# Block-sparse attention and a top-2 mixture of experts: starting the first attention tile head pair by head pair, with the first value sums moved and more value buffers

## The chip, the cores and the metric

One core of one Trainium2 chip (trn2). The metric is device time in microseconds (us) of one execution of the whole program, as the median of three runs.

## The reference

Attention over 4 batches, 8 heads, 768 positions of 64: each query sees its window of keys and, beside it, one summary key (a maximum) and one summary value (a mean) for each block of 32 positions. Its output feeds a router that sends each of the 3072 positions to two of eight experts.

```python
k_sum = k.reshape(B, H, nb, block, D).max(axis=3)
v_sum = v.reshape(B, H, nb, block, D).mean(axis=3)
mask_l = np.abs(pos[:, None] - pos[None, :]) < window
scores_all = np.concatenate([scores_l_m, scores_s], axis=-1)
a = np.exp(scores_all - np.max(scores_all, axis=-1, keepdims=True))
a = a / (np.sum(a, axis=-1, keepdims=True) + 1e-09)
attn_out = np.matmul(a, np.concatenate([v, v_sum], axis=2))
...
h = np.maximum(x[mask] @ w1[e], 0.0)
out[mask] += top2_w[mask, k, None] * (h @ w2[e])
```

## The kernel before, in words

The 3072 positions are 24 tiles of 128 queries, six to a batch. The order of all instructions is written by hand: a loop over t from -2 to 22 (about line 1060 on) issues in each turn, in this order, the scores of tile t + 2 (`mask_sums`, `scores`: TensorE, L308 and L318), their maxima (`smax`: VectorE, L325), the transposes of tile t + 1's exponentials (`p_trans`: TensorE, L341, copied out of PSUM by ScalarE at L344), the exponentials of tile t + 2 (`sexp`: ScalarE, L330 and L333), the product of tile t's weights with the values (`av`: TensorE, L354), the transposes of tile t - 1's output (`x_pe`, L378, copied by `x_copy`, L384), and the division by the sums (`norm`: VectorE, L363 to L369). `at(t, f, ...)` hangs further work between these steps, and `run` issues it: loads of later batches, key maxima, value sums, router and weights. Each engine works through its own list in that order, so an instruction that waits holds up all that is behind it on its engine.

Names that matter here:
- `KB[b % 2]` holds a batch's keys. Batch 0's come in four transfers, one for each pair of heads (L147), behind the queries of tile 0 (`load_q(0)`). `k_head` takes a pair's block maxima (VectorE, L237); later batches' maxima are taken in six pieces (`k_piece`, L231).
- `KX[t % 3]` holds what a tile's scores multiply with: its window of keys (`kx_local`: ScalarE at L122 for tiles 0 and 1, GpSimd at L124 for the others) and the summary keys (`kx_sum`, L130).
- `v_sums(b)` makes a batch's summary values: 48 matrix products in two passes of fp32 (L257), four copies out of PSUM on VectorE (L265 or L267), and for batch 0 copies on GpSimd that put the 24 summary rows into value tiles (L273, L275). `v_rest(b)` fills the others by DMA. For batch 0 it hangs at -0.9, behind tile 0's transposes.
- A tile has two value tiles, one for each half of its queries: one from `VE` (loaded by `load_ve`, L143), and one from `VD` (loaded by `v_load`, L290). `VD` has three buffers in a batch, so `v_load(3)` stands in the loop and waits until tile 0's value product has read the first.
- `warm_up` issues small matrix products whose result nobody reads (L246): `WARM = 100` of them at the start, and 15 between tile 0's transposes.
- SyncE (SP) issues the loads of queries, keys and values, one behind the other. Its transfers use eight semaphores in rotation, so each waits at its issue until the one eight places earlier has landed.

Of the kernel before, what the change touches and what calls it, by code (L numbers as in the profile page):

```python
# [8 lines left out]
F32 = mybir.dt.float32  # L9
# [32 lines left out]
QA = 5  # L42
WARM = 100
SK = HP * NK
# [19 lines left out]
def attn_moe(ctx, tc, qt, kt, vt, wgn, noise, w1, w2, out):  # L64
# [49 lines left out]
    def kx_local(t):  # L114
        b, j = divmod(t, TS)
        k = KB[b % 2][:, :, j * P:j * P + 64 + W]
        n = HP // 2 if t < 1 else HP
        for h in range(0, HP, n):
            for blk in range(2):
                x, y = KX[t % QN][:, h:h + n, blk, L0[blk]:L0[blk] + W], k[:, h:h + n, 64 * blk:64 * blk + W]  # L120
                if t < 2:
                    nc.scalar.activation(x, y, AF.Copy)  # L122
                else:
                    nc.gpsimd.tensor_copy(x, y)  # L124

    def kx_sum(t):
        b, j = divmod(t, TS)
        if j < QN:
            x = KX[t % QN].rearrange("p h b k -> p h (b k)")[:, :, W:W + 2 * NB]
            (nc.gpsimd if b else nc.vector).tensor_copy(x.rearrange("p h (b n) -> p h b n", b=2),  # L130
                                                        KM[b][:, :, None, :].to_broadcast([P, HP, 2, NB]))

    def q_piece(t):
# [4 lines left out]
    VE = [flat[0][:, :TS * VB].rearrange("p (j c) -> p j c", j=TS), keep.tile([P, TS, VB], F32, name="ve")]  # L138
    VD = [[flat[1][:, VB * j:VB * (j + 1)] for j in range(3)],
          [keep.tile([P, VB], F32, name=f"vd{j}") for j in range(2)] + [flat[1][:, 3 * VB:4 * VB]]]  # L140

    def load_ve(b, j):
        nc.sync.dma_start(VE[b % 2][:, j].rearrange("p (h d) -> p h d", h=H), vt[b, j * P:(j + 1) * P])  # L143

    load_q(0)
    for h in range(HP):
        nc.sync.dma_start(KB[0][:, h, PAD:PAD + S], kt[0, :, h])  # L147


# [84 lines left out]
    def k_head(h):  # L234
        if h == 0:
            KM[0] = work.tile([P, HP, NB], F32, name="kmax")
        nc.vector.tensor_reduce(KM[0][:, h], KB[0][:, h, PAD:PAD + S].rearrange("p (n i) -> p n i", i=BLK),  # L237
                                axis=AX.X, op=OP.max)

# [10 lines left out]
    def v_sums(b):  # L250
        if b:
            pt = psum.tile([P, HP, P], F32, name="pt", bufs=2).rearrange("p a b -> p (a b)")
        else:
            pt = psum.tile([P, 2, 512], F32, name="o")[:, 0]
        for j in range(TS):
            for g in range(4):
                nc.tensor.matmul(pt[32 * g:32 * g + NB, 0:C4], ind[:, j, :], VE[b % 2][:, j, C4 * g:C4 * g + C4],  # L257
                                 start=(j == 0), stop=(j == TS - 1), skip_group_check=True)
        x, y = VE[b % 2][W:W + NB], [z[0:NB] for z in VD[b % 2]]
        for g in range(4):  # L260
            i, o = pt[32 * g:32 * g + NB, 0:C4], slice(C4 * g, C4 * g + C4)
            if b == 3 and g % 2:
                nc.scalar.activation(x[:, 0, o], i, AF.Copy)
            elif b:
                nc.vector.tensor_copy(x[:, 0, o], i)  # L265
            else:
                nc.vector.tensor_copy(x[:, 0, o], i)  # L267
        if b == 1:
            nc.gpsimd.tensor_copy(y[0], x[:, 0])
        if b == 0:  # L270
            for i in range(4):
                if i:
                    nc.gpsimd.tensor_copy(x[:, i], x[:, 0])  # L273
                if i < 3:
                    nc.gpsimd.tensor_copy(y[i], x[:, 0])  # L275

    def v_rest(b):
# [3 lines left out]
        if b:  # L281
            for y in VD[b % 2][b == 1:]:
                nc.sync.dma_start(y[0:NB], x[:, 0])
# [3 lines left out]
    def v_load(t):  # L287
        b, j = divmod(t, TS)
        y = VD[b % 2][j % 3].rearrange("p (h d) -> p h d", h=H)
        nc.sync.dma_start(y[NB:NB + VR], vt[b, P * j + 64:P * j + 64 + VR])  # L290
        VX[t] = [VE[b % 2][:, j].rearrange("p (h d) -> p h d", h=H), y]
# [19 lines left out]

    def scores(t):
        s, q, k = SC[t], QR[t], KX[t % QN]
        for hp in range(HP):
            for blk in range(2):
# [20 lines left out]
    def p_trans(t, a):  # L336
        pt = psum.tile([P, HP, P], F32, name="pt", bufs=2)
        for hp in range(HP):
            if t == 0:
                warm_up(1 if a + hp else 8)  # L340
            nc.tensor.transpose(pt[:NK, hp, :], PE_[t][:, a, hp, :], ident)  # L341
# [625 lines left out]

    warm_up(WARM)
    load_q(1)
    for j in range(TS):  # L970
        load_ve(0, j)
    load_q(2)
    v_load(0)
    v_load(1)
    load_q(3)
    v_load(2)
    nc.sync.dma_start(wg32, wgn)
    nc.sync.dma_start(noi, noise)
    load_q(4)
    for h in range(HP):  # L980
        k_head(h)
    q_piece(0)
    q_piece(1)
    at(-0.9, v_sums, 0)
    at(0.8, v_rest, 0)

# [73 lines left out]
    for t in range(-2, NT - 1):  # L1060
# [6 lines left out]
        run(t + 0.03)  # L1067
        if t + 2 < NT:
            mask_sums(t + 2)
            scores(t + 2)  # L1070
# [3 lines left out]
        run(t + 0.5)  # L1074
        if t + 2 < NT:
            smax(t + 2)
        if 0 <= t + 1 < NT:
            p_trans(t + 1, 0)
            p_trans(t + 1, 1)
        if t + 2 < NT:  # L1080
            sexp(t + 2, (0, 1) if t + 3 < NT else (0,))
# [21 lines left out]
        run(t + 0.9)  # L1103
        if 0 <= t and t + 3 < NT:
            v_load(t + 3)
# [598 lines left out]
```

## Time and profile before

| | us |
|---|---|
| median of three runs | 644.94 |
| lowest, highest | 644.83, 646.68 |
| span of the profiled execution | 642.7 |
| the profiled execution's own time | not listed apart; the median is 2.2 above its span |

| engine | busy us, share of the span | instructions |
|---|---|---|
| TensorE (PE) | 621.8 (97%) | 5295 |
| VectorE (DVE) | 481.6 (75%) | 1039 |
| ScalarE (ACT) | 316.0 (49%) | 692 |
| GpSimd (POOL) | 249.0 (39%) | 432 |

The span is the time from the first to the last instruction of one execution that the hardware profiler took. Busy time is a sum over all stages; the attention takes about the first 125 us and the experts the rest. TensorE's busy time has ends that are modelled, so it does not say that TensorE runs at its peak. The times of all rows count from the span's start.

### The profile page before, as it was taken

The page shows a single profiled execution, that of the slowest core. Times are in us where ns is not written, and L with a number is a line of the kernel's source. Part 1 is how long each engine was busy: PE and PEld are TensorE (multiplying, and loading weights), DVE is VectorE, ACT ScalarE, POOL GpSimd, SP SyncE. Part 2 cuts the span into 40 slices and gives each one's busy share as a digit, 9 for nine tenths or more (in the row PEclk, how much of TensorE's full clock was granted, in tenths as well). Part 3 has the DMA queues.
Part 4 walks back from the last instruction along what each step waited for, and adds up shares of the span by engine and source line. Part 5 has one row for each costly group of instructions (what it writes and reads, how often), then busy time and mean ns, then how long its engine had stood idle before and what let it go on. Part 6 is the DMA issues. An engine that isn't in the chain of part 4 may idle for free.

```text
span 642.7 us, 14142 instructions
## 1 busy us (share of the span) xinstructions
PE 621.8 (97%) x5295; PEld 360.3 (56%) x5295; DVE 481.6 (75%) x1039; ACT 316.0 (49%) x692; POOL 249.0 (39%) x432
## 2 busy tenths in 40 slices
PE   8899899899999999999999999999999999999995
PEld 7678777765554554555455544554554455445542
DVE  5848899889797599178878887987898679757510
ACT  4958898852153463065337534654464255425300
POOL 4433044203254433623573256336632542333041
PEclk9989999999999999999999999999999999999999
DMA  9999996678469696636986688779786868763021
GB/s 308 296 294 327 296 303 211 214 265 288 139 200 187 188 221 152 256 91 162 203 245 162 150 212 261 169 139 220 220 199 157 217 202 165 180 193 120 3 95 50
DMA packets 123707, 127.91 MB, mean 199 GB/s; under 512 B 83242, under 2 KB 86674, under 8 KB 123630
## 3 DMA queue, kind: packets, MB, share of 16 engines
q1 hardware_dynamic: 111838, 90.66, 52.9%
q0 software_dynamic: 11792, 36.27, 17.9%
q8 instruction: 43, 0.70, 0.4%
q14 instruction: 34, 0.28, 0.1%
HBM read 81.85 MB, written 25.61 MB: 167 GB/s over the span
## 4 chain that ended last, share of the span: by engine, by line
PE 78%; DVE 11%; ACT 3%; issue 3%; DMA 3%; POOL 0%; POOLq 0%; SPq 0%; DVEq 0%; ACTq 0%
PE pt L1429 29%; PE h L1357 16%; PE h L854 8%; PE pt L909 7%; PE pt L1357 3%; PE o L1357 3%; PE h L909 2%; DVE nm L325 2%; DMA htl<-in_vt_dram 2%; ACT p L333 2%; PE pt L341 1%; PE o L354 1%; PE o L246 1%; PE s L318 1%; DVE y L920 1%
## 5 line engine op out<-in xcount | busy, mean ns | idle before, releaser
L90 POOL DMA_INDIRECT out_dram<-y,tb x52 | 69.3, 1333 | 167.5 <-DVE y L931 129.3
L90 POOL DMA_INDIRECT xg<-xd,tb x54 | 60.4, 1119 | 118.9 <-DVE dsc L653 32.9
L1429 PEld LDWEIGHTS <-hth 128*128 128x128 f16 x576 | 56.4, 98 | 66.7
L931 DVE SCALAR_TENSOR_TENSOR y<-pt,tb,prev 128x512 f32<-128x512 f32 x42 | 31.5, 749 | 65.7 <-PE pt L1429 54.2
L1357 PEld LDWEIGHTS <-w1h 128*128 128x128 f16 x504 | 48.9, 98 | 38.1 <-issue 4.1
L1429 PE MATMUL pt<-w2h,hth 128*128 128x512 f16 x288 | 69.0, 379 | 0.0
L1429 PE MATMUL pt<-w2l,hth 128*128 128x512 f16 x288 | 69.0, 379 | 0.0
L1429 PE MATMUL pt<-w2h,htl 128*128 128x512 f16 x288 | 69.0, 379 | 0.0
L1357 PEld LDWEIGHTS <-w1l 128*128 128x128 f16 x504 | 49.3, 98 | 34.9
L90 POOL DMA_INDIRECT prev<-out_dram,tb x45 | 52.1, 1158 | 24.6 <-issue 12.9
L333 ACT ACTIVATE p<-s,nm 128x120 f32<-128x120 f32 x192 | 50.8, 376 | 0.8
L854 PE MATMUL h<-xte,w1h 128*128 128x384 f16 (+2 forms) x248 | 48.9, 336 | 0.0
L1429 PEld LDWEIGHTS <-htl 128*128 128x128 f16 x288 | 28.2, 98 | 34.0
L1346 ACT ACTIVATE w1h<-stg 128x768 f16<-128x768 f32 (+1 forms) x24 | 22.7, 944 | 40.2 <-DVE stg L1337 40.2
L1389 ACT ACTIVATE hth<-h 128x384 f16<-128x384 f32 (+4 forms) x48 | 23.8, 496 | 35.6 <-PE h L1357 35.6
L1346 ACT ACTIVATE w1l<-stg 128x768 f16<-128x768 f32 (+1 forms) x24 | 22.5, 942 | 37.3 <-DVE stg L1337 37.3
L1357 PE MATMUL h<-xte,w1h 128*128 128x384 f16 (+4 forms) x180 | 39.7, 329 | 0.7 <-DVE h L1383 0.4
L1357 PE MATMUL h<-xte,w1l 128*128 128x384 f16 (+4 forms) x180 | 39.7, 329 | 0.0
L1310 ACT ACTIVATE x<-xt 128x512 f16<-128x512 f32 (+2 forms) x44 | 26.5, 626 | 23.2 <-issue 19.1
L1337 DVE TENSOR_TENSOR stg<-stg 128x256 f32<-128x256 f32 x96 | 36.3, 419 | 0.8
L854 PEld LDWEIGHTS <-w1h 128*128 128x128 f16 x256 | 24.7, 98 | 19.4 <-issue 1.0
L1392 DVE SCALAR_TENSOR_TENSOR htl<-h,hth 128x384 f16<-128x384 f32 (+4 forms) x48 | 26.4, 563 | 11.8 <-ACT hth L1389 11.5
(301 smaller groups left out, 1297.3 us busy)
## 6 DMA issues: line engine op xcount, KB each, us to landing
stg<-in_w_dram SPq DMA_DIRECT2D x64, 512.0 KB
q<-in_qt_dram SPq DMA_DIRECT2D x24, 256.0 KB
xd<-x SPq DMA_DIRECT2D x24, 256.0 KB
out_dram<-xg SPq DMA_DIRECT2D x8, 768.0 KB
kb<-in_kt_dram SPq DMA_DIRECT2D x6, 768.0 KB
hth<-in_vt_dram SPq DMA_DIRECT2D x12, 260.0 KB
htl<-in_vt_dram SPq DMA_DIRECT2D x16, 195.0 KB
ve<-in_vt_dram SPq DMA_DIRECT2D x12, 260.0 KB
```

The source lines that it names most:

```text
L90: return nc.gpsimd.indirect_dma_start(**kw)
L333: nc.scalar.activation(PE_[t][:, a, hp, :], SC[t][:, a, hp, :], AF.Exp, bias=NM[t][:, 1, a, hp:hp + 1], scale=0.125)
L854: nc.tensor.matmul(ph[:, :n], w1_of(w, wn, c, f), x[:, xo + c, c0:c1], start=(k == 0), stop=(k == 11))
L909: nc.tensor.matmul(py, hx[:, f, c * P:c * P + P], wv[:, f, :], start=st, stop=sp)
L931: nc.vector.scalar_tensor_tensor(y, py[:, :d], gw, pv[:, :d], op0=OP.mult, op1=OP.add)
L1310: nc.scalar.activation(t[:r, c:c + k], src, AF.Copy)
L1337: nc.vector.tensor_tensor(o, x, y, op=op)
L1346: nc.scalar.activation(hi, x, AF.Copy, scale=W1S)
L1357: nc.tensor.matmul(ph[:, :h], w[:, la, a, P * j:P * j + P], x[:, j, :h], start=start and k == 0, stop=k == 5, skip_group_check=True)
L1389: nc.scalar.activation(hh[:, f, t], src, AF.Relu)
L1392: nc.vector.scalar_tensor_tensor(hl[:, f, t], src, 0.0, hh[:, f, t], op0=OP.max, op1=OP.subtract)
L1429: nc.tensor.matmul(py, x, wv[:, f, :], start=st, stop=sp, skip_group_check=True)
```

## The change

Seven things change:
- Two pairs of key heads are loaded ahead of tile 0's queries, and the last pair in two halves.
- Tile 0's scores, maxima and exponentials are issued for each head pair (`start`, `start_head`, `start_max`), with its summary keys copied per pair on VectorE. The windows of tile 0 are copied by ScalarE; tile 1's windows and its summary keys, and tile 2's summary keys, go to GpSimd.
- `WARM` falls from 100 to 48; six warm-up products follow each of the first three pairs, and twelve follow tile 2's scores. The 15 between tile 0's transposes go.
- Tile 2's queries are loaded ahead of the values, tile 3's one place earlier.
- `v_sums(0)` moves from -0.9 to 0.1: behind tile 2's scores and tile 1's transposes, ahead of tile 0's value product.
- `VD` has five buffers in batch 0; GpSimd fills all five with the summary rows, eight copies instead of six.
- `v_load(3)` and `v_load(4)` leave the loop and stand at the start, behind tile 4's queries.

```diff
-WARM = 100
+WARM = 48
...
     def kx_local(t):
         b, j = divmod(t, TS)
         k = KB[b % 2][:, :, j * P:j * P + 64 + W]
-        n = HP // 2 if t < 1 else HP
-        for h in range(0, HP, n):
-            for blk in range(2):
-                x, y = KX[t % QN][:, h:h + n, blk, L0[blk]:L0[blk] + W], k[:, h:h + n, 64 * blk:64 * blk + W]
-                if t < 2:
-                    nc.scalar.activation(x, y, AF.Copy)
-                else:
-                    nc.gpsimd.tensor_copy(x, y)
+        for blk in range(2):
+            nc.gpsimd.tensor_copy(KX[t % QN][:, :, blk, L0[blk]:L0[blk] + W], k[:, :, 64 * blk:64 * blk + W])
...
-            (nc.gpsimd if b else nc.vector).tensor_copy(x.rearrange("p h (b n) -> p h b n", b=2),
+            (nc.gpsimd if t else nc.vector).tensor_copy(x.rearrange("p h (b n) -> p h b n", b=2),
...
-    VD = [[flat[1][:, VB * j:VB * (j + 1)] for j in range(3)],
+    VD = [[flat[1][:, VB * j:VB * (j + 1)] for j in (0, 1, 2, 4, 5)],
...
+    VN = (5, 3, 3, 3)
...
-    load_q(0)
     for h in range(HP):
-        nc.sync.dma_start(KB[0][:, h, PAD:PAD + S], kt[0, :, h])
-
+        if h == 2:
+            load_q(0)
+        for c in ((0, S // 2), (S // 2, S)) if h == HP - 1 else ((0, S),):
+            nc.sync.dma_start(KB[0][:, h, PAD + c[0]:PAD + c[1]], kt[0, :, h, c[0]:c[1]])
...
-        nc.vector.tensor_reduce(KM[0][:, h], KB[0][:, h, PAD:PAD + S].rearrange("p (n i) -> p n i", i=BLK),
-                                axis=AX.X, op=OP.max)
+        for n in ((0, NB // 2), (NB // 2, NB)) if h == HP - 1 else ((0, NB),):
+            nc.vector.tensor_reduce(
+                KM[0][:, h, n[0]:n[1]],
+                KB[0][:, h, PAD + BLK * n[0]:PAD + BLK * n[1]].rearrange("p (n i) -> p n i", i=BLK),
+                axis=AX.X, op=OP.max)
+        x = KX[0][:, h].rearrange("p b k -> p (b k)")[:, W:W + 2 * NB]
+        nc.vector.tensor_copy(x.rearrange("p (b n) -> p b n", b=2), KM[0][:, h, None, :].to_broadcast([P, 2, NB]))
+
+    def start_head(h):
+        k_head(h)
+        for blk in range(2):
+            nc.scalar.activation(KX[0][:, h, blk, L0[blk]:L0[blk] + W], KB[0][:, h, 64 * blk:64 * blk + W], AF.Copy)
+        if h == 0:
+            mask_sums(0)
+        scores(0, h, h + 1)
+        if h < HP - 1:
+            warm_up(6)
+        if h:
+            start_max(h - 1)
+
+    def start_max(h):
+        nc.vector.tensor_reduce(NM[0][:, 0, :, h], SC[0][:, :, h], axis=AX.X, op=OP.max)
+        nc.scalar.activation(NM[0][:, 1, :, h], NM[0][:, 0, :, h], AF.Copy, scale=-0.125)
+        for a in range(2):
+            nc.scalar.activation(PE_[0][:, a, h, :], SC[0][:, a, h, :], AF.Exp, bias=NM[0][:, 1, a, h:h + 1],
+                                 scale=0.125)
+
+    def start():
+        NM[0] = work.tile([P, 2, 2, HP], F32, name="nm", bufs=2)
+        PE_[0] = awork.tile([P, 2, HP, NK], F32, name="p")
+        for h in range(HP):
+            start_head(h)
+        start_max(HP - 1)
+        q_piece(1)
...
-            for i in range(4):
-                if i:
+            for i in range(VN[0]):
+                if 0 < i < 4:
                     nc.gpsimd.tensor_copy(x[:, i], x[:, 0])
-                if i < 3:
-                    nc.gpsimd.tensor_copy(y[i], x[:, 0])
+                nc.gpsimd.tensor_copy(y[i], x[:, 0])
...
-        y = VD[b % 2][j % 3].rearrange("p (h d) -> p h d", h=H)
+        y = VD[b % 2][j % VN[b]].rearrange("p (h d) -> p h d", h=H)
...
-            if t == 0:
-                warm_up(1 if a + hp else 8)
...
     load_q(1)
+    load_q(2)
     for j in range(TS):
         load_ve(0, j)
-    load_q(2)
     v_load(0)
+    load_q(3)
     v_load(1)
-    load_q(3)
     v_load(2)
...
-    for h in range(HP):
-        k_head(h)
-    q_piece(0)
-    q_piece(1)
-    at(-0.9, v_sums, 0)
+    v_load(3)
+    v_load(4)
+    at(0.1, v_sums, 0)
...
-        if t + 2 < NT:
+        if t == -2:
+            start()
+        elif t + 2 < NT:
             mask_sums(t + 2)
             scores(t + 2)
...
+        if t == 0:
+            warm_up(12)
...
-        if 0 <= t and t + 3 < NT:
+        if 0 <= t < NT - 3 and t + 3 > 4:
             v_load(t + 3)
```

Three places where rows move. On SP, from tile 4's queries on (q4; `kb1` holds batch 1's keys, `ve` its first value tiles, `htl` the second value tiles of batch 0). Before:

```order
L112 DMA q4_100<-in_qt_dram 128x512
L107 DMA kb1_92<-in_kt_dram 128x4x384
L112 DMA q0_96<-in_qt_dram 128x512
L143 DMA ve_101<-in_vt_dram 128x520 x3
L107 DMA kb1_92<-in_kt_dram 128x4x384
L107 DMA kb0_91<-in_kt_dram 128x4x384
L280 DMA hth_89<-hth_89 24x2x520
L290 DMA htl_90<-in_vt_dram 96x520
```

Now:

```order
L112 DMA q4_100<-in_qt_dram 128x512
L318 DMA htl_90<-in_vt_dram 96x520 x2
L107 DMA kb1_92<-in_kt_dram 128x4x384
L112 DMA q0_96<-in_qt_dram 128x512
L139 DMA ve_101<-in_vt_dram 128x520 x3
L107 DMA kb1_92<-in_kt_dram 128x4x384
L107 DMA kb0_91<-in_kt_dram 128x4x384
L308 DMA hth_89<-hth_89 24x2x520
```

The second value tiles of tiles 3 and 4 have moved ahead of batch 1's keys; tile 3's stood behind all of these.

On TensorE, from tile 0's last transposes (`p_346`, now `p_262`) to tile 0's value product. Before:

```order
L341 MATMUL pt_402<-ident_110,p_346 120x128
L257 MATMUL o_422<-hth_89 24x130 x24
L308 LDWEIGHTS identb_112
L308 MATMUL s_459<-mask0_121,identb_112 64x4x96
...
L318 MATMUL s_459<-kx2_95,q2_98 64x120 x16
L341 MATMUL pt_482<-ident_110,p_412 120x128 x4
L341 MATMUL pt_489<-ident_110,p_412 120x128 x4
L354 MATMUL o_505<-hth_89,pts_400 64x65
```

Now:

```order
L367 MATMUL pt_374<-ident_111,p_262 120x128 x4
...
L336 MATMUL s_392<-mask0_122,identb_113 64x4x96
L346 MATMUL s_392<-kx2_95,q2_98 64x120 x16
L275 LDWEIGHTS identb_113
L275 MATMUL o_191<-identb_113 128x128
...
L367 MATMUL pt_427<-ident_111,p_380 120x128 x4
L367 MATMUL pt_434<-ident_111,p_380 120x128 x4
L286 MATMUL o_450<-hth_89 24x130 x24
L380 MATMUL o_487<-hth_89,pts_372 64x65
```

The value sums (`o<-hth`, 24 rows here, two passes each in the profile) stood ahead of tile 2's mask and scores; now they stand between tile 1's transposes and tile 0's value product.

On GpSimd, the copies of the summary rows (`htl<-hth`, `hth<-hth`) and what stands around them. Before:

```order
L124 COPY kx0_93<-kb0_91 128x4x96 x2
L275 COPY htl_90<-hth_89 24x520
L273 COPY hth_89<-hth_89 24x520
...
L124 COPY kx1_94<-kb0_91 128x4x96 x2
```

Now:

```order
L118 COPY kx1_94<-kb0_91 128x4x96 x2
L124 COPY kx1_94<-kmax_263 128x4x48
L118 COPY kx2_95<-kb0_91 128x4x96 x2
L124 COPY kx2_95<-kmax_263 128x4x48
L118 COPY kx0_93<-kb0_91 128x4x96 x2
L303 COPY htl_90<-hth_89 24x520
...
L303 COPY htl_90<-hth_89 24x520 x2
L118 COPY kx1_94<-kb0_91 128x4x96 x2
```

Tile 1's windows and the summary keys of tiles 1 and 2 have come in ahead, and two summary-row copies more stand before tile 4's windows (`kx1<-kb0`, the last row of both).

## Rows read from the trace of the kernel before

**Rows 1.** Windows: busy us of PE, PEld, DVE, ACT, POOL; PEclk; DMA share; GB/s.
```profile
140.00:160.00 20.00, 20.00 (x137) 11.07 (x135) 18.97 (x64) 5.33 (x11) 6.13 (x11) 1.00 0.89 310
```

**Rows 2.** Chain of waits, 0 to 70 us: start us, us, what.
```profile
1.55 7.41 PE o L246 x100
...
14.46 1.46 PE o L257 x48
...
18.05 1.09 PE o L354 x32
...
21.79 10.41 DMA htl<-in_vt_dram
...
32.25 1.93 PE o L354 x30
34.18 1.05 PE pt L378 x4
...
36.61 1.02 PE pt L341 x8
...
38.72 0.59 PE pt L378 x4
...
40.76 0.29 PE s L308 x4
41.05 0.82 PE s L318 x32
...
42.35 0.90 issue
...
66.33 1.63 issue
```

**Rows 3.** Windows, the start and the stall at tile 3.
```profile
1.50:5.00 3.50, 3.45 (x33) 3.46 (x34) 1.91 (x14) 0.54 (x1) 2.72 (x17) 1.00 0.85 289
5.00:9.00 4.00, 4.00 (x74) 3.90 (x71) 3.56 (x4) 1.51 (x5) 2.62 (x11) 1.00 1.02 388
30.00:32.20 2.20, 0.00 (x0) 0.00 (x0) 2.20 (x5) 2.17 (x9) 0.88 (x3) 1.00 1.03 267
32.20:34.10 1.90, 1.85 (x30) 1.74 (x30) 0.25 (x1) 0.44 (x2) 0.66 (x2) 0.54 1.10 303
34.10:36.60 2.50, 2.50 (x42) 1.92 (x42) 1.06 (x3) 0.60 (x1) 0.00 (x0) 0.67 1.05 270
```

**Rows 4.** Timeline of DVE: start us, us, instruction, count [idle before, releaser].
```profile
6.09 2.91 DVE L237 TENSOR_REDUCE kmax<-kb 128x24 f32<-128x768 f32 x3 [0.39 <-DMA kb<-in_kt_dram]
...
10.53 1.16 DVE L325 TENSOR_REDUCE nm<-s 128x8 f32<-128x960 f32 x1 [1.07 <-PE s L318]
...
15.99 1.21 DVE L267 COPY hth<-o 24x130 f32<-24x130 f32 x4 [3.07 <-PE o L257]
...
27.29 0.69 DVE L231 TENSOR_REDUCE kmax<-kb 128x16 f32<-128x512 f32 x1 [1.26 <-DMA kb<-in_kt_dram]
```

**Rows 5.** Timeline of POOL, the copies of summary rows and what follows them.
```profile
17.32 0.62 POOL L275 COPY htl<-hth 24x520 f32<-24x520 f32 x1 [5.79 <-issue]
...
21.36 2.75 POOL L124 COPY kx<-kb 128x384 f32<-128x384 f32 x6
```

**Rows 6.** Timeline of ACT, exponentials of tiles 0 and 1 and the copies between.
```profile
11.96 2.12 ACT L333 ACTIVATE p<-s,nm 128x120 f32<-128x120 f32 x8
13.92 1.17 ACT L344 ACTIVATE pts<-pt 120x512 f32<-120x512 f32 x2
...
15.22 2.12 ACT L333 ACTIVATE p<-s,nm 128x120 f32<-128x120 f32 x8
```

**Rows 7.** The page's DMA issues: out<-in, engine, count, KB each.
```profile
htl<-in_vt_dram SPq DMA_DIRECT2D x16, 195.0 KB
```

**Rows 8.** Timeline of SP's queue, eight places behind batch 1's last value load.
```profile
36.00 0.35 SPq L373 DMA_DIRECT2D xd<-x  x1
```

**Rows 9.** DMA queues between 64 and 68 us: packets, MB, share of 16 engines.
```profile
q8 instruction: 1, 0.02, 1.8%
```

More of the change, by code (lines that the diff above doesn't have):

```diff
@@ L258, in v_sums @@
                                  start=(j == 0), stop=(j == TS - 1), skip_group_check=True)
-        x, y = VE[b % 2][W:W + NB], [z[0:NB] for z in VD[b % 2]]
+        x, y = VE[b % 2][W:W + NB], [z[0:NB] for z in VD[b % 2][:VN[b]]]
         for g in range(4):
@@ L281, in v_rest @@
         if b:
-            for y in VD[b % 2][b == 1:]:
+            for y in VD[b % 2][b == 1:VN[b]]:
                 nc.sync.dma_start(y[0:NB], x[:, 0])
@@ L310, in mask_sums, with scores @@
                                  skip_group_check=True)
-    def scores(t):
+    def scores(t, h0=0, h1=HP):
         s, q, k = SC[t], QR[t], KX[t % QN]
-        for hp in range(HP):
+        for hp in range(h0, h1):
             for blk in range(2):
@@ L1074, in attn_moe @@
         run(t + 0.5)
-        if t + 2 < NT:
+        if t == 0:
+            warm_up(12)
+        if -2 < t < NT - 2:
             smax(t + 2)
@@ L1079, in attn_moe @@
             p_trans(t + 1, 1)
-        if t + 2 < NT:
+        if -2 < t < NT - 2:
             sexp(t + 2, (0, 1) if t + 3 < NT else (0,))
```

## The prediction

> **What bounds the kernel now.** I read the windows by stage first: between 140 and 160 us TensorE is busy for 20.00 of 20 us [rows 1]. From there on a start that comes earlier by some time should end earlier by about as much. So the question is what the change does to the first 40 us, and whether it survives until 140.
>
> For the first 40 us I read the chain of waits [rows 2]. The reader is to see three things. The 100 warm-up matmuls stand in it for 7.41 us, then tile 0's scores, maxima and transposes follow. The value sums of batch 0 take 1.46 us at 14.46, and straight behind them come mask and scores of tile 2, so that tile 0's value product (L354) starts at 18.05. And the longest piece is a transfer: tile 3's second value tile, 10.41 us from its issue at 21.79 to 32.25. [...]
>
> The profiled execution has no time of its own listed; its span of 642.7 us lies 2.2 us under the median of 644.94, and I put my differences on that median.
>
> **Part 1: tile 0 by head pairs.** The last key head landed when DVE's run of reduces ended: three reduces in 2.91 us from 6.09, so the fourth ran from about 8.05 to 9.00 [rows 4]. The same bytes (four heads and one q tile) still stand ahead of that landing, so it doesn't move. Now DVE has in front of the last half head: the third head (about 7.05 to 8.0), a copy, one head pair's maximum (a quarter of 960 columns; between 0 and the 1.16 us of a whole one, I take 0.4, in proportion with some fixed cost), two half reduces (0.55 each; between 0.48, half of 0.97, and 0.97). That ends at 9.6. Tile 1's sums go to POOL (192 columns; between 0 and the 0.62 of POOL's copy of 520, I take 0.35, in proportion with some fixed cost) [rows 5], so tile 1's scores start at 10.0 and end at 11.2 with mask and scores of 0.29 and 0.82 [rows 2]: as early as before, no more. What moves is tile 0's exponentials: all done at about 11.4, where they ended at 14.08 before (11.96 and 2.12) [rows 6]. Its eight transposes then take 1.02 us behind tile 1's scores, with no warm-ups between them, to 12.3. ACT's copies of them (1.17) end at 13.0. Tile 1's exponentials ended 2.25 behind such copies (15.09 to 17.34), so now at 15.3 against 17.34 [rows 6]. **Gain here: 2.0 us.**
>
> The warm-ups cost nothing. Only 33 matmuls fitted into 1.5 to 5.0 and 74 in the next 4 us [rows 3], so TensorE doubled its rate at about 5; the clock column shows 1.00 in both, I go by the spacing. 48 warm-ups end near 5.9, and q tile 0 lands there as well. Six more behind each of three heads and twelve behind tile 2's scores (0.06 each) run while TensorE would wait for DVE or ACT.
>
> **Part 2: value sums behind tile 2's scores.** TensorE now takes tile 2's scores at 12.3 to 13.5, tile 1's transposes as the exponentials come, to 15.5, then the sums (1.46) to 17.0. Behind them nothing is left to hide what follows: four DVE copies (1.21) to 18.3 and POOL's first copy (0.62) to 19.0 [rows 4, 5]. Before, scores and transposes of tiles 2 and 1 covered just that. Tile 0's value product starts at 19.1 instead of 18.05, TensorE standing idle for 2 us ahead of it. **The 2.0 us are gone and 1.1 more are lost.** POOL makes eight value copies where it made six; at six in 4.04 us (17.32 to 21.36) [rows 5] it is free at 23.8, and tile 4's first keys are there at 24.3, which costs up to 0.2 us more. So tiles 1 and 2 run about 1.2 us later than before.
>
> **Part 3: five buffers.** Tile 3's and tile 4's second value tiles are now issued right behind q tile 4, ahead of batch 1's keys, and have nothing to wait for. The stall at tile 3 goes. TensorE had reached it at 29.9; now it gets there at 30.9 to 31.0 and goes on at once: 1.09 us at full clock, done at 32.0 instead of 34.18, **2.2 us earlier**. What is late next is DMA work put behind the two loads, 390 KB [rows 7] or 1.0 to 1.5 us at the 388 to 267 GB/s shown [rows 3]. DVE's key maximum waited for batch 1's second half until 27.29 [rows 4]; at 28.5 it still ends ahead of tile 3's value product, which needs DVE's norm of tile 2 by 30.9. Batch 1's last value load had landed by 36.00, when SP issued the transfer eight places behind it [rows 8]; it then has one load (195 KB, 0.7 us) more ahead of it, 36.7, and TensorE wants it at about 36.5.
>
> **Part 4: the clock.** Transposes, mask and scores behind the stall took 2.43 us (34.18 to 36.61) where the same took 0.59, 0.29 and 0.82 later [rows 2]: without the fall another 0.7 us. I count half, 0.35, since only one execution shows the fall. DVE takes back 0.25 in front of tile 6's maximum, where batch 2's key maxima stand.
>
> **Sum:** 2.2 + 0.35 - 0.25 = 2.3 us at tile 6. From there to 140 us the order of work is the old one. **Forecast 642.6 us.**
>
> **The rivals.**
> *DMA sets the pace.* The share of the DMA engines is 1.02 to 1.10 in these stretches [rows 3], and the change sends the same bytes. If the last value load of batch 1 had landed just before its use at 39.31 (38.72 and 0.59) [rows 2], the gain is gone: 644.9, up to 0.7 more. Against it stands SP's row at 36.00 [rows 8].
> *The clock falls in the new gap.* TensorE was idle for over 2.2 us when it fell before [rows 3]; the new gap at 17 to 19 us is 2.0. The two slow stretches lost 0.46 of 1.9 and 0.33 of 2.5 us, 1.7 us in all. Put on tiles 0 to 2, it leaves 0.6 of the gain: 644.3. For it speaks the similar length, against it that the sums right before it keep TensorE busy, where before the stall it had little.
> *Slower: instruction fetch.* TensorE stood for 0.90 us at 42.35 and for 1.63 us at 66.33 in the midst of one tile's matmuls, with no releaser but "issue" [rows 2], and around the second the DMA queue that carries instructions moved one packet of 0.02 MB [rows 9]. If such packets stand in line behind full queues, tiles that run closer together meet more of them. It decides from three more stalls of 1.63 on: 642.6 + 4.9 = 647.5. Against it: two in 30 us of full queues. [...]
> *More than forecast.* One of these two stalls goes as TensorE's instructions shift: 641.0, and 640.3 with all of the clock's 0.7.
>
> **How the numbers follow.** Forecast 0.55, DMA 0.17, clock 0.15, fetch 0.08, more 0.05. A difference of 0.3% (1.93 us) is about what a measurement of this kernel can tell from none: faster means under 643.0, slower over 646.9. The forecast's own spread, 641.4 to 643.6 from the bounds of part 1, the half-counted clock and the 1.0 to 1.5 us of DMA, gives 0.46 to faster and 0.09 to same; "more" gives 0.05 to faster, the clock 0.03. DMA goes to same but for 0.01, the clock's other 0.12 to same, fetch to slower: 0.54, 0.37, 0.09. The range leaves fetch and the outer tenth of the rest out: 640.3 to 645.4.
>
> **What would show it.** Right: tile 0's exponentials end near 11.4; a gap of about 2 us between the value sums and tile 0's value product, which starts near 19; no wait at tile 3's; tile 6's scores end near 34. Wrong: L354 of tile 0 starts before 18; a DMA wait at DVE's key maxima or at batch 1's value sums; a granted clock under 1 around 19 us; a gain at 36 us that is no longer there at 140.

## The result, and the profile after

The change takes **649.21 us** (nine runs, 646.85 to 652.35) against 644.94 of nine runs of the kernel before: a ratio of 1.0072, 95% interval 1.0049 to 1.0095. That is 0.7% slower, where the forecast was 642.6. The profiled execution took 648.33 us with a span of 646.6; the span of the kernel before was 642.7. One execution of a later kernel, h1_copy_first, took 1175.36 us at a granted clock of 0.794 and is left out of that kernel's numbers.

The chain of waits of the changed kernel, first 24 us (start us, us, what). L275 are the warm-ups, L346 a head pair's scores, L255 its maximum, L256 and L258 its scaling and exponentials, L245 a key copy, L303 GpSimd's first value copy, L380 a value product:

```profile
1.55 5.08 PE o L275 x48
...
7.56 0.41 PE s L346 x8
...
8.00 0.42 DVE nm L255
...
8.44 0.22 ACT nm L256
...
8.68 0.61 ACT p L258 x2
9.29 0.35 ACT kx L245 x2
9.64 0.05 issue
9.69 0.47 PE s L346 x8
...
10.94 0.61 ACT p L258 x2
11.55 0.35 ACT kx L245 x2
11.90 0.05 issue
11.95 0.50 PE s L346 x8
...
21.89 0.62 POOL htl L303
22.52 0.04 issue
22.56 1.37 PE o L380 x30
```

Follow one turn: the second head pair's scores end at 7.97, then the first pair's maximum, scaling and two exponentials run, then the third pair's key copy, and only then, at 9.69, come the third pair's scores. The fourth's start at 11.95: **2.26 us a head pair**, where VectorE needs 0.97 for a pair's reduction (2.91 for three) [rows 4]. The chain alternates between three engines, one of them at work at a time. ScalarE's rows show where this leaves tile 0 and tile 1 (start us, us, engine, line, operation, in brackets the idle time before and what ended it):

```profile
14.55 0.61 ACT L258 ACTIVATE p<-s,nm 128x120 f32<-128x120 f32 x2
...
16.54 2.12 ACT L361 ACTIVATE p<-s,nm 128x120 f32<-128x120 f32 x8
```

Tile 0's exponentials end at 15.16 and tile 1's at 18.66; before, at 14.08 and 17.34 [rows 6]. TensorE's rows of the next step:

```profile
18.96 1.53 PE L286 MATMUL o<-hth 128*24 128x130 f32 x48
21.83 0.33 PE L380 MATMUL o<-hth,pts 120*64 120x65 f32 x2 [1.33 <-DVE hth L296]
22.56 0.27 PE L380 MATMUL o<-htl,pts 120*64 120x65 f32 x1 [0.40 <-POOL htl L303]
```

The value sums end at 20.49 and tile 0's value product gets going at 22.56, 4.5 us behind the 18.05 of before [rows 2]. Between the two lie 2.07 us; two of the products already run at 21.83, so TensorE stands idle for 1.33 and for 0.40 of them. Windows of the same execution (window, us, busy time and instructions of PE, PEld, DVE, ACT and POOL, granted clock, DMA share, GB/s):

```profile
15.00:20.00 5.00, 5.00 (x100) 4.06 (x104) 1.50 (x2) 4.77 (x16) 0.00 (x0) 1.00 1.09 244
20.00:25.00 5.00, 3.27 (x76) 2.64 (x68) 2.13 (x7) 1.92 (x8) 2.89 (x5) 0.83 1.05 330
25.00:30.00 5.00, 5.00 (x100) 4.20 (x96) 3.50 (x7) 2.98 (x11) 4.73 (x10) 0.83 1.07 353
```

In this execution TensorE's granted clock is 0.83 from 20 to 25 us, where that pause lies, and 0.83 in the 5 us behind; the fall that the kernel before had behind 32 us (0.54 and 0.67) [rows 3] is gone: in those two windows it is 1.00 now. So is the 10.41 us transfer at tile 3 [rows 2]: from 15 to 120 us TensorE waits for no DMA any more, where it waited 2.3 us for this one before.

Two marks tell how far the late start reaches: VectorE's maximum of tile 6 and of tile 23, the last. First the kernel before, then the change:

```profile
36.79 1.16 DVE L325 TENSOR_REDUCE nm<-s 128x8 f32<-128x960 f32 x1 [1.45 <-PE s L318]
...
121.37 1.15 DVE L325 TENSOR_REDUCE nm<-s 128x8 f32<-128x960 f32 x1
```

```profile
38.92 1.15 DVE L353 TENSOR_REDUCE nm<-s 128x8 f32<-128x960 f32 x1
...
121.48 1.16 DVE L353 TENSOR_REDUCE nm<-s 128x8 f32<-128x960 f32 x1
```

2.1 us late at tile 6, level at tile 23. Read from these two executions alone, the late start is absorbed and the loss comes later. One part of it does lie at the very end. The last row of the chain, first of the kernel before, then of the change:

```profile
636.99 0.71 POOL out_dram L90
```

```profile
638.92 0.71 POOL out_dram L90
```

From the end of this transfer to the end of the span it was 5.0 us (637.70 to 642.7) and is now 7.0 (639.63 to 646.6). In the trace's records GpSimd ends the branch around the overflow code (L1679, L1651 before) with a semaphore and drains its queue behind it. Between the starts of the semaphore and of the drain lay 0.09 us before (637.54 and 637.63); 2.59 lie there now (639.47 and 642.06). It is not the branch itself that got longer: from the branch to the semaphore it takes 0.48 us in both. The order of work there is unchanged; GpSimd's program has five instructions more in front of it (764 records against 759). Of the 3.9 us between the two spans, 0.1 thus stand at tile 23's maximum and 2.0 in this tail; the other 1.8 lie between the two (from that maximum to the end of the last transfer it was 516.3 us and is 518.1).

### The profile page after: what moved, and what is told of

It reads as the page before. It is cut to its first block, busy times and chain, and to the rows that moved or that the text cites. A ratio compares the mean times of both kernels' runs of the same rounds, so it can differ in the third digit from the quotient of the medians.

```text
span 646.6 us, 14093 instructions
## 1 busy us (share of the span) xinstructions
PE 621.9 (96%) x5258; PEld 359.6 (56%) x5258; DVE 482.4 (75%) x1044; ACT 316.3 (49%) x697; POOL 252.4 (39%) x438
## 4 chain that ended last, share of the span: by engine, by line
PE 72%; DVE 10%; issue 6%; ACT 5%; POOL 3%; DMA 2%; SPq 1%; POOLq 0%; DVEq 0%; ACTq 0%
PE pt L1457 29%; PE h L1385 16%; PE h L880 5%; PE pt L935 5%; PE o L1385 3%; PE pt L1385 3%; PE h L935 2%; ACT p L361 2%; DVE nm L353 2%; POOL xg L90 2%; PE o L380 1%; PE pt L367 1%; POOL out_dram L90 1%; DMA xg<-xd,tb 1%; PE s L346 1%
## 5 line engine op out<-in xcount | busy, mean ns | idle before, releaser
L361 ACT ACTIVATE p<-s,nm 128x120 f32<-128x120 f32 x184 | 48.7, 376 | 0.8
```

What stands on the lines that cost most here:

```text
L361: nc.scalar.activation(PE_[t][:, a, hp, :], SC[t][:, a, hp, :], AF.Exp, bias=NM[t][:, 1, a, hp:hp + 1], scale=0.125)
```

## The experiments

**Theory A**: the late start is absorbed, and the loss is the position of the code: engines stop for instructions at other places, GpSimd at its jump above all. **Theory B**: the late start carries to the end, and its apparent absorption is chance between two executions. **Theory C**: all of it is chance. Ratios are to runs of the kernel before on the same chip, 95% intervals in brackets.

**e1_pool5: five instructions on GpSimd, nothing else.**

```diff
     nc.gpsimd.memset(XG[3], 0.0)
+    pad = const.tile([P, 4], F32, name="pad")
+    for i in range(5):
+        nc.gpsimd.memset(pad[:, 0:1], 0.0)
```

> The kernel before with nothing but five one-column memsets added on GpSimd while it is idle in the first 10 us, so that GpSimd's program is as much longer as it is in the change (754 + 5 recorded instructions). Theory A (position of the code): the change lost about 2 us in the tail, because GpSimd's jump past the overflow branch then has to wait for an instruction fetch (2.6 us from the branch's last semaphore to the drain where it was 0.1); the same must happen here, and the time is 2.0 us above the kernel before, with the work up to the last matmul unmoved. Theory B (the late start of the change carries to the end): nothing is late here, so the time is that of the kernel before within 0.5 us. Theory C (chance from execution to execution): no difference either.

646.79 us, 1.0023 (1.0002 to 1.0044). The last row of its chain, against a span of 643.6:

```profile
636.18 0.71 POOL out_dram L90
```

6.7 us of tail. The semaphore and the drain lie 2.39 us apart. Five one-column memsets in the first 10 us bring this at 637 us, so GpSimd's number of instructions alone does it (764 records against 759; the expectation's 754 is wrong). The interval of the time reaches down to almost nothing; it is the gap that shows the effect.

**e2_count: the old order with the change's instruction counts.**

```diff
-WARM = 100
+WARM = 63
...
+    for i in range(8):
+        nc.vector.memset(pad[:, 1:2], 0.0)
+    for i in range(6):
+        nc.scalar.activation(pad[:, 2:3], ones[:, 0:1], AF.Copy)
...
+    for i in range(2):
+        nc.sync.dma_start(pad2[0:1, i:i + 1], noise[0:1, 0, i:i + 1])
```

(and e1's five memsets)

> The kernel before, its order of work untouched, with every engine's number of instructions made that of the change before 15 us: 63 warm-up matmuls in place of 100 (TensorE 74 rows fewer), five GpSimd memsets, eight VectorE memsets, six ScalarE copies of one column, two DMAs of one element. Theory A: the stalls of the change at 124 us (about 1 us), at 520 us (about 1.3 us) and in the tail (2 us) come back without its new order: 3 to 4.5 us above the kernel before. Theory B: the start is as early as before, so no difference, 0.5 us at most. Theory C: no difference of its own.

647.84 us, 1.0049 (1.0025 to 1.0073), with a tail of 6.95 us. It falls short of A's range (2.8 us above by the medians, 3 to 4.5 expected) and lies well above B's; its interval overlaps e1's, so that code on the other engines costs anything beside this gap is not shown by it. Its start was also somewhat later than intended (tile 6's maximum at 37.57).

**e3_pool_less: the change, GpSimd's count as before.** Five small constants move to VectorE.

```diff
-    nc.gpsimd.tensor_scalar(base8, base8, HALF, None, op0=OP.subtract)
+    nc.vector.tensor_scalar(base8, base8, HALF, None, op0=OP.subtract)
...
```

(likewise the copy into `bs`, both writes of `tie`, the subtraction on `iotar`)

> The change with five of GpSimd's small constants made by VectorE, so that GpSimd has as many instructions as in the kernel before. Theory A: GpSimd's jump in the tail takes 0.1 us again in place of 2.6, and the time falls by 2.0 us against the change, to about 1.7 to 2.3 us above the kernel before; the stalls at 124 and 520 us stay, unless VectorE's five instructions move one of them. Theory B: five small instructions in the first 4 us change nothing: 0.7% above the kernel before, as the change is.

647.12 us, 1.0034 (1.0009 to 1.0059). The tail is 5.1 us again, semaphore and drain 0.09 apart. So about 2 us of the loss go with that gap, **and about as much stays**: the change has a second cost.

**e4_five: part 3 alone.**

```diff
-    VD = [[flat[1][:, VB * j:VB * (j + 1)] for j in range(3)],
+    VD = [[flat[1][:, VB * j:VB * (j + 1)] for j in (0, 1, 2, 4, 5)],
...
     load_q(4)
+    v_load(3)
+    v_load(4)
```

> The kernel before with part 3 of the change alone: five buffers for the second value tile and both early loads; head pairs, value sums and warm-ups as before. GpSimd makes two more copies (2 instructions more, fewer than the five). Theory A: the stall at tile 3 goes, tile 6's maximum starts about 2 us earlier than in the kernel before, and by 100 us none of this is left, since VectorE is full from 70 to 120 us; at the end between 0.5 us less and 1 us more than the kernel before, by where instruction fetches fall. Theory B: what is gained at tile 6 stays: 1.5 to 2.3 us under the kernel before.

644.85 us, 0.9987 (0.9965 to 1.0009): at most 0.35% faster, perhaps nothing. The stall is gone from its profile, yet nothing that can be measured is gained. Why, e1 and e2 show: they have the old order too. Chain of waits of e1_pool5 at tile 3, then of e2_count:

```profile
25.60 1.08 PE o L357 x30
26.68 1.32 issue
28.00 0.28 PE o L357 x2
```

```profile
22.30 0.74 PE o L358 x21
23.04 10.06 DMA htl<-in_vt_dram
33.10 0.04 issue
33.15 1.15 PE o L358 x30
```

e2 waits for the same transfer as the kernel before; e1, which differs from that kernel in five memsets alone, doesn't: its tile has the value rows in time, and tile 6's maximum starts at 34.60, 2.2 us ahead of the 36.79 of the kernel before. (The 1.32 us in e1 are one of TensorE's stops, told of in the last section.) **The wait that part 3 removes is there in one execution and not in another.**

The next four test the start. f1 delays it with the old code, f2 to f4 undo part 2 and the loop of part 1 in e3, singly and together.

**f1_late.**

```diff
         for i in range(n):
-            nc.tensor.matmul(VO[0][:, i % 2, 0:P], identb, identb, start=True, stop=True, skip_group_check=True)
+            x = ident if n == WARM and i >= 30 else identb
+            nc.tensor.matmul(VO[0][:, i % 2, 0:P], x, x, start=True, stop=True, skip_group_check=True)
```

> The kernel before with 70 of its 100 warm-up matmuls in float32 in place of bfloat16, about 0.07 us longer each, and no instruction more or fewer on any engine: the first scores start about 4 us later, everything behind is as before. Theory A (the start is absorbed by tile 12, since the change was 2.1 us late at tile 6 and level at 100 us): 0 to 1 us above the kernel before. Theory B (a late start carries to the end, and what looked like absorption was one execution of the kernel before against one of the change): 3 to 4.5 us above it.

650.46 us, 1.0112 (1.0079 to 1.0145). The delay came out larger than meant, and the count did move: a float32 matmul is recorded as two, with two weight loads (170 warm-ups in the chain, 140 rows more), and the warm-ups take 19.66 us where they took 7.41 [rows 2], about 0.175 us more for each of the 70 (expected 0.07). Tile 6's maximum starts at 44.75, 8.0 us late, tile 23's 5.3 us late, and the median is 7.3 us up. A has no room for that.

**f2_sums_back.**

```diff
-    at(0.1, v_sums, 0)
+    at(-0.9, v_sums, 0)
...
-        if t == 0:
+        if t == -1:
             warm_up(12)
```

> The change with GpSimd's count as in the kernel before (as in e3_pool_less) and with part 2 undone: batch 0's value sums behind tile 0's transposes again, the twelve warm-ups there too. The pause of 2 us ahead of tile 0's value product goes, and with it the fall of the granted clock at 23 to 27 us; tile 0's product starts 1.5 to 2 us earlier than in the change (22.56), tile 6's maximum as well. Theory A: this is absorbed, time as e3_pool_less (0.3% above the kernel before). Theory B: 1.5 to 2.5 us under e3_pool_less, level with the kernel before.

645.43 us, 1.0024 (1.0004 to 1.0044). Tile 0's value product starts at 20.50, as expected. The granted clock still falls, but earlier (0.66 from 10 to 15 us). The time is nearer to A's 0.3% than to B's, and its interval holds e3's value as well as almost nothing: by itself this run decides nothing.

**f3_kx_pool and f4_both.** f4 is f3 with f2's edit. In both, three writes of `caps` move to VectorE too, so that GpSimd has 760 records.

```diff
-            nc.scalar.activation(KX[0][:, h, blk, L0[blk]:L0[blk] + W], KB[0][:, h, 64 * blk:64 * blk + W], AF.Copy)
+            x, y = KX[0][:, h, blk, L0[blk]:L0[blk] + W], KB[0][:, h, 64 * blk:64 * blk + W]
+            if h < 2:
+                nc.scalar.activation(x, y, AF.Copy)
+            else:
+                nc.gpsimd.tensor_copy(x, y)
...
+        if h:
+            start_max(h - 1)
         scores(0, h, h + 1)
...
-        if h:
-            start_max(h - 1)
```

> e3_pool_less with the loop of tile 0 broken up: key copies of heads 2 and 3 on GpSimd in place of ScalarE, so that none stands behind exponentials, and each head's maximum issued ahead of the next head's scores; part 2 as in the change. If that loop (2.26 us a head) was what held tile 0, its exponentials end at 11.4 to 12.5 in place of 15.16 and tile 0's value product starts near 20 in place of 22.56. Theory A: time as e3_pool_less. Theory B: 2 us under it.

> e3_pool_less with both: loop broken up and value sums back ahead of tile 2's scores. Tile 0's value product starts at 16 to 17, 1 to 2 us ahead of the kernel before (18.05), where the forecast had 19.1 and the change 22.56. Theory A: no faster than the kernel before. Theory B: 1 to 2.5 us under the kernel before, which would make it the fastest of these.

646.24 us, 1.0032 (1.0011 to 1.0053), and 644.93 us, 1.0020 (0.9999 to 1.0041). The loop did not break: tile 0's exponentials end at 15.32 and 14.96, its value product starts at 24.09 and 21.61. TensorE's rows of f3_kx_pool say why (L352 scores, L262 exponentials):

```profile
9.03 0.44 PE L352 MATMUL s<-kx,q 64*64 64x120 f32 x8 [0.99 <-ACT p L262]
...
13.20 0.68 PE L352 MATMUL s<-kx,q 64*64 64x120 f32 x8 [0.77 <-ACT p L262]
```

A head pair's scores wait for the *exponentials of the one before*, which they don't need. All four stand in one PSUM tile (one buffer for TensorE's results), and the dependence holds the tile, not a quarter of it: 0.99 and 0.77 us of idle time in these two rows. The key copies in ScalarE's list were only half of the loop.

**g1_two_tiles: f2 with tile 0's scores in two PSUM tiles.**

```diff
-        NM[0] = work.tile([P, 2, 2, HP], F32, name="nm", bufs=2)
...
+        if h % 2 == 0:
+            SC[0] = gate_space()[:, :, :SK // 2].rearrange("p a (h k) -> p a h k", h=2)
+            S2.append(SC[0])
...
+        nm = work.tile([P, 2, 2, 2], F32, name="nm2", bufs=2)
+        nc.vector.tensor_reduce(nm[:, 0], S2[i], axis=AX.X, op=OP.max)
```

> f2_sums_back with tile 0's scores in two PSUM tiles, heads 0 and 1 in the first, 2 and 3 in the second, each with its own maximum and exponentials. Theory D (in the change and in f3_kx_pool the heads waited for one another because all four stand in one PSUM tile and a dependence holds the tile: a head's scores wait for the exponentials of the head before): tile 0's exponentials end at 11.4 to 12.2, as the forecast had it, in place of 14.9, and tile 0's value product starts near 16 in place of 20.50. About six tenths of a shift at tile 0 have reached tile 23 in the runs so far, so 0.5 to 2 us under the kernel before. Rival E (the landing of the keys, about 1 us a head, or VectorE holds tile 0): the exponentials end after 13.5, and the time is that of f2_sums_back, 0.2% above the kernel before.

645.16 us, 1.0009 (0.9982 to 1.0035). Exponentials end at 13.71: 0.2 us past the 13.5 of rival E, well behind D's 11.4 to 12.2. The time lies between what the two have and decides for neither. ScalarE's rows, then TensorE's (L274 exponentials of two head pairs, L245 key copy, L259 scores):

```profile
9.69 1.11 ACT L274 ACTIVATE p<-s,nm 128x120 f32<-128x120 f32 x4
10.68 0.47 ACT L245 ACTIVATE kx<-kb 128x96 f32<-128x96 f32 x2
```

```profile
11.03 0.49 PE L259 MATMUL s<-kx,q 64*64 64x120 f32 x6 [1.15 <-ACT kx L245]
```

The scores no longer wait for exponentials, but the last head pair's still wait for a key copy behind them. h1 takes that away.

**h1_copy_first.**

```diff
+        if h == 3:
+            start_max(0)
         k_head(h)
...
-        if h >= 2:
-            start_max(h - 2)
+        if h == 3:
+            start_max(1)
```

(in g1, with the key copies ahead of both)

> g1_two_tiles with the key copy of the last head ahead of the first two heads' exponentials in ScalarE's order (in g1 it stood behind them, ended at 11.1, and the last head's scores waited for it). Theory D (heads wait for one another only by the order of ScalarE's list and by the shared PSUM tile, and both are gone now): tile 0's exponentials end at 12.6 to 13.1 in place of 13.71 (14.08 in the kernel before), its value product at about 18 where no instruction fetch comes between. Theory B, six tenths carried: 0 to 1 us under g1 (0.1% above the kernel before), so level with the kernel before to 0.1% under it; no theory has it faster than the kernel before by more than 1.5 us.

645.39 us, 0.9997 (0.9978 to 1.0017): level with the kernel before, no better. Exponentials end at 13.39, a little behind D's 12.6 to 13.1 and still 2 us behind the forecast's 11.4: the third head pair's keys land at 7.8, and VectorE then has two reductions (the last in halves) and a maximum to do. And the gain in front was lost at once. Chain of g1_two_tiles, then of h1_copy_first, at tile 2's scores:

```profile
16.01 0.20 PE s L360 x6
16.21 1.04 issue
17.25 1.03 PE s L360 x26
```

```profile
15.68 0.20 PE s L362 x6
15.88 2.73 issue
18.62 1.03 PE s L362 x26
```

**g2_late22 and g3_change_again.** g2 is f1 with 22 float32 warm-ups (`i >= 78`), g3 the change once more.

> f1_late with 22 float32 warm-ups in place of 70, so that tile 0's value product starts at about 21.7 as in the change (21.83; 17.98 in the kernel before), with the code of the kernel before and its count on every engine. In f1_late 11.9 us of delay at tile 0 were 5.3 at tile 23 and 7.3 in the median. Theory B (a good part of the late start carries): 1.5 to 3 us above the kernel before; with the 1.5 to 2 us of GpSimd's jump that is the whole of the change's loss. Theory A (absorbed by tile 12; the rest of the loss is the position of TensorE's, VectorE's and ScalarE's code): 0 to 0.8 us above it.

> The change once more, beside the others on one chip. Both theories: 3.5 to 5 us above the kernel before. Its profile shows whether the level start at tile 12 (68.64 against 68.56) was one execution's chance: theory B has it 1 to 3 us late there, theory A level again; GpSimd's jump in the tail takes 2.4 to 2.6 us by both.

g2: 648.50 us, 1.0045 (1.0021 to 1.0069). Tile 0's value product starts at 21.32, about as meant, but its chain has a stop of 2.22 us at 29.95, so that tile 6's maximum starts only at 40.96; tile 23's at 122.85. Its TensorE code is 44 rows longer, so its 3.5 us, somewhat more than B's 1.5 to 3, are not the delay's alone by proof; A's 0.8 us are excluded. g3: 648.73 us, 1.0052 (1.0021 to 1.0082), tail 6.85 us. Its tile 6 starts earlier than in the first execution of the change, and tile 23 too. In between stands tile 12's maximum, for which theory B had 1 to 3 us of delay. It starts at 68.22, level with the 68.56 of the kernel before: in this B missed.

```profile
37.92 1.15 DVE L353 TENSOR_REDUCE nm<-s 128x8 f32<-128x960 f32 x1
...
68.22 1.16 DVE L353 TENSOR_REDUCE nm<-s 128x8 f32<-128x960 f32 x1 [0.40 <-PE s L346]
...
121.05 1.16 DVE L353 TENSOR_REDUCE nm<-s 128x8 f32<-128x960 f32 x1
```

All profiles together (start of the two maxima, their distance, and the tail from the end of the last GpSimd transfer to the end of the span):

| kernel | tile 6 | tile 23 | between | tail | ratio |
|---|---|---|---|---|---|
| e1_pool5 | 34.60 | 119.43 | 84.8 | 6.7 | 1.0023 |
| e4_five | 35.05 | 119.12 | 84.1 | 5.3 | 0.9987 |
| g1_two_tiles | 36.66 | 119.29 | 82.6 | 5.2 | 1.0009 |
| before | 36.79 | 121.37 | 84.6 | 5.0 | 1 |
| f2_sums_back | 37.40 | 119.10 | 81.7 | 5.5 | 1.0024 |
| e2_count | 37.57 | 120.70 | 83.1 | 7.0 | 1.0049 |
| g3_change_again | 37.92 | 121.05 | 83.1 | 6.9 | 1.0052 |
| h1_copy_first | 38.20 | 122.30 | 84.1 | 5.1 | 0.9997 |
| the change | 38.92 | 121.48 | 82.6 | 7.0 | 1.0072 |
| f4_both | 39.20 | 123.25 | 84.1 | 5.3 | 1.0020 |
| e3_pool_less | 40.26 | 123.64 | 83.4 | 5.1 | 1.0034 |
| g2_late22 | 40.96 | 122.85 | 81.9 | 5.4 | 1.0045 |
| f3_kx_pool | 42.88 | 126.09 | 83.2 | 5.3 | 1.0032 |
| f1_late | 44.75 | 126.69 | 81.9 | 5.3 | 1.0112 |

From tile 6 to tile 23 it takes 81.7 to 84.8 us **wherever it begins**. The kernel before, at 84.6, was near the slow end of that scatter and the change, at 82.6, near the fast one; that alone made 2.1 us of lateness look absorbed. Over a range of 10 us in the second column some 2 us are absorbed, not more.

A good part of the scatter can be seen in the chains. TensorE stops now and then with no releaser but "issue"; the last section says what these stops are. Behind tile 6 the kernel before had two, 0.90 and 1.63 us [rows 2], the second right in front of tile 12's maximum. The first execution of the change has none above 0.6 us from there to tile 23, and f1 and f2, with 81.9 and 81.7 us, have none either. So it was the kernel before that came late to tiles 12 and 23 in its execution, more than that the change made its delay good.

So theory B holds for the start and theory A for the tail; by the middle values of e1 and e3 each has about half. The stretch from tile 23's maximum to the last transfer takes 515.9 to 519.0 us in the 14 executions, in no order that goes with the changes, so the 1.8 us that lie there between the first two profiles are within its scatter.

## Why the prediction was wrong

**What bounds the kernel** stood: a start that shifts, shifts the end.

**Part 1 is the step that failed.** It had tile 0's exponentials "all done at about 11.4"; they ended at 15.16. The forecast added up each engine's own work on a head pair (DVE's reductions, half a microsecond for a maximum) and let the pairs overlap. In the code they can't: the key copy of a pair stands behind an earlier pair's exponentials in ScalarE's list, and all pairs share a PSUM tile. Each row was priced well (a pair's maximum 0.42, taken as 0.4; the scores of the last pair behind its reductions), but the waits between rows were not followed round. Head by head cost 2.26 us a pair. With the loop taken out in g1 and h1 the exponentials end at 13.4 to 13.7, so even then 11.4 was not to be had: the third pair's keys, whose reduction the forecast put at about 7.05, landed at 7.7 to 7.8 there.

**Part 2** had the price right and the place wrong: 2.1 us from the end of the value sums to the value product, forecast (17.0 to 19.1) and measured (20.49 to 22.56). All 3.5 us between 19.1 and 22.56 came from part 1.

**Part 3** went as said in the trace, and the value rows no longer hold a tile up. Its 2.2 us were mis-sized: they are what one execution waited. e2 waits for the same transfer, e1 doesn't, and part 3 alone brings 0.13% with an interval that holds nothing and 0.35%. The prediction counted a wait for a DMA at its full length from one profile.

**Part 4**: the fall of the clock behind tile 3 went (0.54 and 0.67 before, 1.00 now), but another came. It is not tied to the new pause: the first execution of the change has it at 20 to 30 us (0.83 in both windows), the second, with the same pause, at 10 to 15. Windows of g3_change_again:

```profile
10.00:15.00 5.00, 3.61 (x52) 2.94 (x50) 3.05 (x7) 2.79 (x11) 2.45 (x6) 0.67 1.06 334
...
20.00:25.00 5.00, 3.27 (x87) 2.60 (x80) 2.30 (x8) 1.86 (x8) 2.95 (x5) 1.00 1.06 306
```

The rival that put a fall in the pause was thus right for one execution of two, and its price of 1.7 us is inside what the start lost anyway. The 0.25 us taken back at tile 6's maximum had no row behind them, and no run shows them.

**The sum.** "From there to 140 us the order of work is the old one" was true, and the lateness went through it. The tail was not looked at: the sum put it at nothing without a reason, and it held half of the loss. The rival of instruction fetch had 0.08 and priced three more stops of TensorE. In the change's first execution both of the stops that it named were gone, where the last rival counted on one going; that is luck of the execution (g3, the same program, has 0.60 us at 45.52), and the kernel was slower all the same. The 640.3 of that last rival counts half of the clock's 0.7 twice (641.0 less the other half is 640.6), which decides nothing here.

The two costs as measured by ratios: 0.23% for the five instructions (e1), 0.34% for the change without them (e3), 0.57% together, against 0.72% and 0.52% for the change in its two measurements. Their intervals are wide (0.02 to 0.44% and 0.09 to 0.59%), so halves are as exact as this gets. That the parts' shares of the 0.34% lie with the loop and the exposed sums is argued from the traces: undoing the sums (f2, 1.0024), then the loop (g1, 1.0009; h1, 0.9997) points that way step by step, but neighbouring intervals overlap. Theory C falls with e1 and e3: the tails are 6.7 to 7.0 us in all four executions with five instructions more on GpSimd and 5.0 to 5.5 in the ten with none to two.

No kernel here beats the one before by more than the measurement can tell.

## What to carry to other kernels

Before pricing a pipeline of small pieces, walk once round its loop, through every engine's list and every shared buffer: a piece is as long as the longest cycle, not as its longest engine (here 2.26 us a head pair, against VectorE's 0.97). A wait for a transfer in one profile is one draw: look at another execution of the same order before counting its removal in full. And where a program ends in a branch around code that rarely runs, a change in an engine's number of instructions can move the end: five more on GpSimd made this tail 1.2 to 2.0 us longer. Compare the tails of two profiles, and the stops marked "issue", before looking for the cause of a small difference anywhere else.

## What the runs showed of the hardware

Behind GpSimd's branch around the overflow code the drain started 0.09 us after the semaphore with 759 to 761 recorded instructions on that engine, and 2.4 to 2.6 us after it with 764. GpSimd's branch itself takes 0.48 us to the semaphore in all 14 executions; the stop lies one instruction further. The same branch on VectorE takes 2.9 to 3.3 us and on ScalarE 2.4 to 2.7, in the kernel before as in all others. For GpSimd the runs show that the cost comes with five instructions; what it waits for is not shown.

TensorE also stops in the middle of straight code, with no releaser but "issue", at a place that belongs to its program. With the TensorE code of the kernel before it was behind the third transpose of tile 6 in three executions: 0.90 us in the kernel before [rows 2], 1.54 in e1_pool5 and 0.99 in e4_five. With the code of g1 and h1 it was behind the sixth matmul of tile 2's scores, 1.04 and 2.73 us; in f2, with four matmuls fewer in front, behind the tenth, 0.54 us.

The traces show what these places have in common. Count TensorE's records (weight loads, matmuls and semaphores) from the start: the stop at tile 6 comes after number 1473, the one at tile 2's scores after number 449, which is four times 256 less. In the first 130 us of the 14 executions 26 times 0.85 us or more pass from one weight load to the next without a semaphore to wait for. All 26 lie at 449 or a multiple of 256 behind it, to within one record, whatever work stands there. The DMA queue "instruction" (q8) moves one packet of 16 KB for each such step, and in all 26 cases TensorE goes on 1.2 to 1.7 us after the packet's end (in the kernel before at 43.24 and 67.96, with ends at 41.78 and 66.73); at none of the other steps does it go on sooner than 1.2 us after it. So these stops are read here as waits for instructions, and how long one is goes with the time at which its packet lands: at the same place of the same TensorE code, two matmuls ahead of the end of a value product, the stop took 0.21 us in the kernel before (up to 26.72) and 1.32 in e1_pool5 (up to 28.00).

Most of some 250 such steps have no such stop; these 26 do. The DMA engines were busy around the stops (share 1.03 in the kernel before from 40 to 45 us, 1.07 and 1.08 in g1 and h1 from 15 to 19), but the change's first execution has shares of 1.05 to 1.09 from 15 to 30 us and no such stop, so busy DMA engines alone don't make one.
